# Bit masks in eight wide operations, one chunk's inverse over 128 partitions, a square on ScalarE, and a new stated order

## The chip, the cores and the metric

The kernel runs on one core of a Trainium2 chip. The metric is the device time of one execution in microseconds (us). The engines are PE (TensorE, matrix products; PEld is its weight load), DVE (VectorE), ACT (ScalarE), POOL (GpSimd) and SP (SyncE, which here only issues transfers).

## The reference

Delta-rule attention over 32 sequences (4 batches of 8 heads, 768 positions, head dimension 48), whose output, laid out as 4 x 768 x 384, passes through a normalised MLP with a residual:

```python
k_n = k / (np.linalg.norm(k, axis=-1, keepdims=True) + 1e-06)
for t in range(S):
    kt, vt, bt = (k_n[:, :, t], v[:, :, t], beta[:, :, t, None])
    y[:, :, t] = np.einsum('bhd,bhde->bhe', q[:, :, t], state)
    v_old = np.einsum('bhde,bhd->bhe', state, kt)
    state = state + bt[:, :, :, None] * np.einsum('bhd,bhe->bhde', kt, vt - v_old)
# x = y as (B, S, H*D), D = 384, hidden 1536
xn = (x - mu) / np.sqrt(var + 1e-06) * g_ln
out = x + np.maximum(xn @ w_ch1, 0.0) @ w_ch2
```

Everything is fp32.

## The kernel before

**Chunks.** The 768 positions are cut into 12 chunks of C = 64. Within a chunk the recurrence becomes matrix products, once a unit triangular 64 x 64 matrix, built from the products of the keys (`gram`, gsb) and beta, has been inverted for every head. The state then goes from chunk to chunk (`recur`: L979, L996 or L1013, L1020, L1030), and the chunk's 256 rows of output go through the MLP (`mlp`: first L1322 and L1337 for chunk 0, later L1296, L1217 and L1419).

**Two ways of inverting.** Chunk 0 is inverted by doubling (`first_inverse`): blocks of 1, 2, 4, ... 32 rows are joined in five levels. Each level, for each of two groups of heads, is a product E on PE (L720), a masked copy of its result on DVE (`copy_predicated`, L727), a product Z on PE (L737), two transposes on DVE (L685) and copies back on ACT (L679). The masks say which elements a level joins: one 128 x 64 mask for each of six bit numbers, made at the start on DVE from GpSimd's index ramps `xor` and `bits`. Before the levels, the norms of the keys are taken (`first_norms`: square L594, sum L595, square root L596, L597 to L602 for -beta / norm^2), the product of the keys is scaled by them (L693), masked (L702) and transposed (L708).

The other chunks are inverted by rows on DVE (`rows_inverse`), two chunks at a time with 128 partitions, one partition for each 32 x 32 block of each head; chunk 1 goes alone, on 64 partitions. Step j multiplies column j of the inverse by row j of the matrix (L856, into tmp) and subtracts (L863): 31 steps, with `n * w` elements each. The blocks come through DRAM (gsb to gd on SP, gd to gb, and at the end xb to xd and xd to xt); ACT and DVE take norms from the diagonal (L835 to L840) and scale (L846). Two 32 x 32 blocks are joined to 64 x 64 by `join` (transpose L884, products L894 and L900).

**Weights.** Both weight matrices come as 64-bit words in twelve pieces of 768 KB, fetched by ACT's queue into five buffers (`fetch`) and put together from their two halves by ACT (L524, L532), DVE (L529) and GpSimd (L542).

**The order.** Every step is recorded with `add` together with what it reads and writes. `emit` then writes the steps in the order of a list of step numbers, `ORDER`; a "z" in it stands for a matmul of zeros (L1511). Each engine executes its part of that list strictly in order (`in_this_order`), so an instruction that waits holds all behind it on its engine, transfers that it issues included.

```python
        for n in stated_order():
            if n < 0:
                self.filler()
                continue
            fn, deps = self.steps[n]
            fn()
```

ScalarE needs a table of functions for each set of activations; the build places a load in front of the first activation that needs another set. A square root of a constant (L439) is recorded early.

Of the kernel before, what the change touches and what calls it, by code (L numbers as in the profile page):

```python
# [9 lines left out]
I32 = mybir.dt.int32  # L10
# [6 lines left out]
C = 64  # L17
DP = 64
BK = 32
FB = 32  # L20
# [43 lines left out]
146 232 230 149 326 150 219 669 154 z 209 234 155 156 208 231 233 210 158 157 251 46 235 164 160 162 327 200 161 328 239 201 411 159 413 165 170 166  # L64
# [136 lines left out]
def kernel(  # L201
# [78 lines left out]
    masks = [small[:, i].bitcast(I32) for i in range(6)]  # L280
    xor, bits, eye, brow = small[:, 6].bitcast(I32), small[:, 7].bitcast(I32), small[:, 8], small[:, 9]
    bnat = sb("bnat", [128, GH])
    beta_f = sb("beta_f", [64, FB])
    beta_b = sb("beta_b", [128, NSL, BK])
    g_sb = sb("g_sb", [128, KC])
    eps = sb("eps", [128, 1])
# [843 lines left out]
    def cap(i):  # L1130
        return CAP[i]
# [517 lines left out]
```

## Time and profile before

| | |
|---|---|
| runs | 507.06, 510.91, 511.09 us (median 510.91) |
| profiled execution | 506.83 us, span 505.1 us |
| granted clock of PE, mean | 0.973 |
| busy: PE, PEld | 485.9 us (96%), 445.7 us (88%) |
| busy: DVE, ACT, POOL | 355.2 us (70%), 249.0 us (49%), 275.7 us (55%) |
| moved by transfers | 54.99 MB, 109 GB/s |
| costliest on DVE | L863 73.7 us (186 instructions), L856 73.1 us (186), L1237 63.6 us (96) |
| costliest on PE | L1419 109.5 and 84.5 us, L1296 50.2 us |

A stretch's row gives its length and then, for each engine, the busy time and the number of instructions, then PE's granted clock as a share of full speed and the busy share of the transfer engines. A row of the timeline gives start, duration, engine, line, operation, output and input, count, and in brackets the idle time before it with what ended it. Matmuls are pipelined, so that PE's busy time is the time in which something was in it.

### The profile page before, as it was taken

Reading aid. Unit: us, or ns where it says so; the run is one execution under the profiler, and the core shown is the slowest. Engines: PE = TensorE matmul, PEld = TensorE weight load, DVE = VectorE, ACT = ScalarE, POOL = GpSimd, SP = SyncE. Lnnn points to the kernel's source line nnn. Section 1 sums busy time; section 2 is a strip of 40 time slices with the busy share of each in tenths; the row PEclk is TensorE's granted clock in tenths of the full one; section 3 lists DMA queues with packets and bytes.
Section 4 is the critical chain, followed back from the end, with each engine's and each line's share of the span. In section 5 each row is a group of like instructions: output and inputs, shape, how many; then the busy total and the mean of one; then the engine's idle time right before and its main releaser. Section 6 shows DMA issues by size and latency. Waiting matters only on the chain.

```text
span 505.1 us, 22184 instructions
## 1 busy us (share of the span) xinstructions
PE 485.9 (96%) x9606; PEld 445.7 (88%) x9606; DVE 355.2 (70%) x774; ACT 249.0 (49%) x620; POOL 275.7 (55%) x430
## 2 busy tenths in 40 slices
PE   6777999999999999999999999999999999999996
PEld 3666988688988898899999999999999999999996
DVE  9689987997699458886559898478899238143251
ACT  5777772633645434636444544436563347363230
POOL 5464527255754595629893462591642851645643
PEclk9776799999999999999999999999999999999999
DMA  8979896756646676448734434765245412111101
GB/s 173 308 153 187 270 189 79 107 138 133 90 87 106 192 127 114 46 100 205 155 41 64 102 55 153 150 91 87 57 85 136 82 23 58 43 50 46 31 12 31
DMA packets 196097, 54.99 MB, mean 109 GB/s; under 512 B 186076, under 2 KB 189404, under 8 KB 196000
## 3 DMA queue, kind: packets, MB, share of 16 engines
q1 hardware_dynamic: 189920, 40.58, 42.1%
q10 hardware_dynamic: 3872, 9.83, 6.1%
q0 software_dynamic: 2208, 3.17, 3.7%
q8 instruction: 75, 1.23, 1.0%
q14 instruction: 22, 0.18, 0.1%
HBM read 36.64 MB, written 16.91 MB: 106 GB/s over the span
## 4 chain that ended last, share of the span: by engine, by line
PE 78%; DVE 13%; SPq 3%; issue 2%; POOL 1%; DMA 1%; ACT 1%; ACTq 0%; DVEq 0%; POOLq 0%
PE f L1419 31%; PE f L1217 22%; PE f L1296 6%; DVE xb L863 4%; DVE tmp L856 4%; SPq L349 3%; PE by L1020 2%; PE two L1013 2%; PE by L979 2%; PE by L771 2%; PE two L979 2%; PE two L1030 1%; PE two L771 1%; PE by L894 1%; PE by L900 1%
## 5 line engine op out<-in xcount | busy, mean ns | idle before, releaser
L1406 POOL TENSOR_TENSOR h_all<-h_all 128x256 f32<-128x256 f32 x123 | 90.2, 746 | 133.3 <-PE f L1419 103.7
L1419 PE MATMUL f<-w_sb,h_all 128*128 128x192 f32 x492 | 109.5, 332 | 0.0
L1419 PE MATMUL f<-words,h_all 128*128 128x192 f32 x396 | 84.5, 330 | 0.3 <-POOL h_all L1406 0.3
L1419 PEld LDWEIGHTS f<-w_sb,h_all 128*128 128x128 f32 x492 | 81.8, 190 | 1.8 <-DVE o L1437 0.2
L863 DVE TENSOR_TENSOR xb<-xb,tmp 128x87 f32<-128x87 f32 (+21 forms) x186 | 73.7, 396 | 4.8
L856 DVE TENSOR_TENSOR tmp<-xb,gb 128x87 f32<-128x87 f32 (+21 forms) x186 | 73.1, 393 | 4.9
L1237 DVE TENSOR_TENSOR h_all<-h_all,f 128x512 f32<-128x512 f32 x96 | 63.6, 682 | 14.2 <-PE f L1217 13.1
L1419 PEld LDWEIGHTS f<-words,h_all 128*128 128x128 f32 x396 | 66.6, 190 | 1.7 <-POOL h_all L1406 1.0
L1296 PE MATMUL f<-xnt,w_sb 128*128 128x256 f32 x216 | 50.2, 382 | 0.0
L349 POOL DMA_DIRECT2D tb<-in_k_dram x64 | 41.9, 660 | 10.3 <-DVE kt L751 9.4
L1239 ACT ACTIVATE h_all<-h_all 128x512 f32<-128x512 f32 x48 | 28.5, 624 | 34.4 <-DVE h_all L1237 34.0
L1296 PEld LDWEIGHTS f<-xnt,w_sb 128*128 128x128 f32 x216 | 40.2, 190 | 5.2
L1233 ACT COPY h_all<-f 128x512 f32<-128x512 f32 x48 | 26.3, 590 | 33.9 <-PE f L1217 17.1
L1437 DVE TENSOR_TENSOR o<-f,x 128x192 f32<-128x192 f32 x33 | 11.6, 352 | 41.8 <-PE f L1419 25.9
L1217 PE MATMUL f<-words,w_sb 128*128 128x128 f32 x256 | 31.7, 276 | 0.0
L1305 ACT ACTIVATE h_all<-f 128x256 f32<-128x256 f32 x36 | 13.4, 383 | 34.8 <-PE f L1296 34.8
L1217 PEld LDWEIGHTS f<-words,w_sb 128*128 128x128 f32 x256 | 30.0, 192 | 0.2
L1217 PE MATMUL f<-xnt,w_sb 128*128 128x128 f32 x192 | 25.4, 276 | 0.0
L542 POOL TENSOR_TENSOR w_sb<-words 128x768 uint32<-128x768 uint32 (+1 forms) x11 | 15.0, 1364 | 17.7 <-DVE words L529 16.7
L1217 PEld LDWEIGHTS f<-xnt,w_sb 128*128 128x128 f32 x192 | 23.7, 192 | 0.1
L1322 PEld LDWEIGHTS f<-xnt,w_sb 128*128 128x128 f32 x144 | 19.5, 203 | 3.4 <-ACT h_all L1330 0.2
L1084 ACT ACTIVATE xnt<-xnt,g_sb 128x256 f32<-128x256 f32 x27 | 12.5, 499 | 19.2 <-DMA xnt<-xld 19.1
(246 smaller groups left out, 955.0 us busy)
## 6 DMA issues: line engine op xcount, KB each, us to landing
words<-in_moe_w_ch_dram ACTq DMA_DIRECT2D x10, 768.0 KB, 7.8
gd<-gsb SPq DMA_DIRECT2D x11, 512.0 KB, 3.9
v<-in_v_dram SPq DMA_DIRECT2D x24, 192.0 KB, 4.2
kr<-in_k_dram SPq DMA_DIRECT2D x46, 96.0 KB, 3.9
out_dram<-o SPq DMA_DIRECT2D x44, 96.0 KB, 2.4
xld<-xlt SPq DMA_DIRECT2D x9, 384.0 KB, 3.0
xnt<-xld SPq DMA_DIRECT2D x36, 96.0 KB, 3.3
gb<-gd SPq DMA_DIRECT2D x44, 64.0 KB, 3.0
```

The source lines that it names most:

```text
L349: add(eng, cost, lambda: QUEUE[eng].dma_start(out=out_, in_=in_), r, w, bulk=n * ns / 16e3, **kw)
L856: lambda j=j, n=n, w=w, t=t: nc.vector.tensor_tensor(out=t, in0=xv[:, 0:n, j : j + 1].to_broadcast([np_, n, w]), in1=gv[:, j : j + 1, j + ...
L863: "DVE", dve(n * w), lambda t=t, rest=rest: nc.vector.tensor_tensor(out=rest, in0=rest, in1=t, op=ALU.subtract),
L979: nc.tensor.matmul(dst[half(e), hp, j], src[drows(hp), (e if n else key_half(c, hp, e)) * GP + j], s_all[drows(hp), e, j], start=(n == 0 o ...
L1217: nc.tensor.matmul(wide(p[:, 128 * n : 128 * n + 128]), w[n // 2][:, n % 2 * 128 : n % 2 * 128 + 128], r, start=start and n == 0, stop=Tru ...
L1233: add("ACT", act(512), lambda: nc.scalar.copy(o, p), pk, ok)
L1237: add("DVE", dve(512), lambda: nc.vector.tensor_tensor(out=o, in0=o, in1=p, op=op), pk, ok)
L1239: add("ACT", act(512), lambda: nc.scalar.activation(o, o, ACTF.Relu), [], ok)
L1296: nc.tensor.matmul(p[:, 0:TOK], w1_sb[:, t, f * 128 : (f + 1) * 128], xnt[:, t], start=(t == 0), stop=(t == KC - 1))
L1322: nc.tensor.matmul(p[:, 0:128], w1_sb[:, t, f * 128 : (f + 1) * 128], xnt[:, t, cols], start=(t == 0), stop=(t == KC - 1))
L1406: add(eng, cost, lambda: e.tensor_tensor(out=out_, in0=x, in1=y, op=op), r, w, port=2 if eng == "Pool" else 1, pr=-2)
L1419: lambda f=f, t=start and f == 0: nc.tensor.matmul(p[:, 0:D2], lhs(f), rhs[:, f], start=t, stop=(f == F2 - 1), skip_group_check=True),
```

## The change

Four parts. Code lines that are only moved are left out.

**Masks.** The two index ramps are laid out so that one 32-bit word holds a column's or row's own bits in its upper half and the exclusive-or in its lower half; a shift by the bit number, an AND and a compare then give a mask. Mask 0 is made by itself, masks 1 to 5 together on 320 columns.

**Chunk 1 on 128 partitions** (`ways=2`): partitions 64 to 127 hold a second copy of the 64 blocks; of the inverse's rows the even ones are kept in the lower and the odd ones in the upper half, so a step has about half the elements. The second copy comes by one transfer gb to gb, and beta for it by two more loads, issued on ACT's queue. The result goes back by eight transfers instead of four.

**Norms:** (norm + 1e-6)^2 is an activation with a bias on ACT instead of a product on DVE.

**Order:** `ORDER` is another list throughout.

```diff
-    beta_f = sb("beta_f", [64, FB])
+    beta_f = sb("beta_f", [128, FB])
...
+    rows_, both, steps = flat[:, 960:1024], flat[:, 832:960].rearrange("p (n t) -> p n t", t=C), flat[:, 800:806]
+    wide = flat[:, 0 : 6 * C].rearrange("p (n t) -> p n t", t=C)
+    c_pool(lambda: nc.gpsimd.iota(steps, pattern=[[1, 6]], base=0, channel_multiplier=0), 0.15, ["steps"])
...
-    for n in MASKED:
-        k_, m, w = n, masks[n], C
-        t1, t2 = (flat[:, C * i : C * i + w] for i in (2 * n, 2 * n + 1))
...
-                out=t1, in0=xor[:, 0:w], scalar1=w - 1, scalar2=k_, op0=ALU.bitwise_and, op1=ALU.logical_shift_right
...
-                out=t2, in0=own, scalar1=k_, scalar2=1, op0=ALU.logical_shift_right, op1=ALU.bitwise_and
...
-                out=m, in0=t1, scalar=1, in1=t2, op0=ALU.is_equal, op1=ALU.mult
...
+    for n, (own, key) in enumerate(((bits, "bits"), (rows_, "rows"))):
...
+                out=both[:, n], in0=own, scalar=16, in1=xor, op0=ALU.logical_shift_left, op1=ALU.bitwise_or
...
+    for n in range(2):
+        ns_ = slice(0, 1) if n == 0 else slice(1, 6)
...
+                out=wide[:, ns_], in0=both[:, n : n + 1].to_broadcast([128, m_, C]),
+                in1=steps[:, ns_, None].to_broadcast([128, m_, C]), op=ALU.logical_shift_right,
...
+                out=wide[:, ns_], in0=wide[:, ns_], scalar1=65536 + C - 1, scalar2=None, op0=ALU.bitwise_and
...
+                out=small[:, ns_].bitcast(I32), in0=wide[:, ns_], scalar1=65537, scalar2=None, op0=ALU.is_equal
...
             add("ACT", 0.21, lambda ss=ss, nr=nr: nc.scalar.sqrt(nr, ss), ks, kn_, **kw)
+            add("ACT", 0.21, lambda nr=nr, nd=nd: nc.scalar.activation(nd, nr, ACTF.Square, bias=eps), kn_ + ["eps"], kd, **kw)
             add("DVE", 0.17, lambda nr=nr: nc.vector.tensor_scalar_add(nr, nr, 1e-6), [], kn_, port=2, **kw)
-            add("DVE", 0.17, lambda nr=nr, nd=nd: nc.vector.tensor_tensor(out=nd, in0=nr, in1=nr, op=ALU.mult), kn_, kd, port=1, **kw)
...
-    def rows_inverse(L, chunks, beta_l, xd, **kw):
-        np_ = C * len(chunks)
-        gv, xv, tv = gb[0:np_], xb[0:np_], tmp[0:np_]
+    def rows_inverse(L, chunks, beta_l, xd, ways=1, **kw):
+        own = C * len(chunks)
+        np_, LA = own * ways, L // ways
+        gv, xv, tv = gb[0:np_], xb[0:np_, 0:LA], tmp[0:np_]
...
+        if ways > 1:
+            dma("SP", gb[own:np_], gb[0:own], own, 168, [("gb", n) for n in range(4)], [("gb", 4)], **kw)
...
+        for q in range(ways):
+            pq = slice(own * q, own * q + own)
...
+                    out=xv[pq].rearrange("p s t -> p (s t)")[:, q :: L + ways], in_=db[pq, q::ways]
...
-            n, w = j + 1, L - 1 - j
+            n, w = j // ways + 1, L - 1 - j
...
+            for q in range(ways):
+                dma(
+                    "SP", xts[c % NX][rows.start + q : rows.stop : ways, :, cols],
+                    xdv[own * q + p0 : own * q + p0 + GH].rearrange("h s t -> s h t"),
...
+    for e in range(2):
+        dma(
+            "ACT", beta_f[C + e * FB : C + (e + 1) * FB],
+            beta[2 * e : 2 * e + 2, :, C : 2 * C].rearrange("g h (b t) -> b (g h) t", t=FB),
...
-    rows_inverse(FB, (1,), (beta_f, [("beta_f", e) for e in range(2)]), 1, pr=-20)
+    rows_inverse(FB, (1,), (beta_f, [("beta_f", e) for e in range(4)]), 1, ways=2, pr=-20)
```

What the new order does on the engines in the front part of the program:

- ACT: before, the only table load stands in front of L439, which is ACT's first activation. Now a load stands in front of the first copy L426 and another in front of the first square root L596, and L439 comes after the two new squares. The first fetch of weights follows the second L596 instead of preceding both.
- DVE: mask 0 and the two `both` words come before the sums L595, the shift and AND for masks 1 to 5 after them, their compare after the second group's L708. L846 comes after the last L727 of the first group instead of ahead of it.
- PE: E of the second group (L720) comes ahead of Z of the first (L737) in the first level; the eight transposes of the queries come after the second level's first product; the third level's first product comes ahead of the second level's last. There are two zero products instead of one, and the eight transposes of chunk 3's keys (L568) stand ahead of the first L1322 instead of behind it.
- POOL: the identity matrix is finished after the beta loads and two memory operations; the second beta row is loaded after both beta_f parts.
- SP: the transfer gb to gb follows the four loads gd to gb of chunk 1, ahead of three loads of chunk 2's keys.

More of the change, by code (lines that the diff above doesn't have):

```diff
@@ L386 @@
     )
-    c_dve(
-        lambda: nc.vector.tensor_tensor(out=flat[:, 960:1024], in0=xor, in1=bits, op=ALU.bitwise_xor), 0.22, ["rows"], ["xor", "bits"], port=1,
-    )
     MASKED = (0, 1, 2, 3, 4, 5)
-    for n in MASKED:
-        k_, m, w = n, masks[n], C
-        t1, t2 = (flat[:, C * i : C * i + w] for i in (2 * n, 2 * n + 1))
+    for n, (own, key) in enumerate(((bits, "bits"), (rows_, "rows"))):
         c_dve(
-            lambda t1=t1, k_=k_, w=w: nc.vector.tensor_scalar(
-                out=t1, in0=xor[:, 0:w], scalar1=w - 1, scalar2=k_, op0=ALU.bitwise_and, op1=ALU.logical_shift_right
+            lambda n=n, own=own: nc.vector.scalar_tensor_tensor(
+                out=both[:, n], in0=own, scalar=16, in1=xor, op0=ALU.logical_shift_left, op1=ALU.bitwise_or
@@ L397 @@
             ),
-            0.17, [("ma", n)], ["xor"], port=2,
+            0.22, [("both", n)], [key, "xor"], port=1,
         )
-        own = flat[:, 960 : 960 + w] if n else bits[:, 0:w]
+    for n in range(2):
+        ns_ = slice(0, 1) if n == 0 else slice(1, 6)
+        m_ = ns_.stop - ns_.start
         c_dve(
-            lambda t2=t2, k_=k_, own=own: nc.vector.tensor_scalar(
-                out=t2, in0=own, scalar1=k_, scalar2=1, op0=ALU.logical_shift_right, op1=ALU.bitwise_and
+            lambda n=n, ns_=ns_, m_=m_: nc.vector.tensor_tensor(
+                out=wide[:, ns_], in0=both[:, n : n + 1].to_broadcast([128, m_, C]),
+                in1=steps[:, ns_, None].to_broadcast([128, m_, C]), op=ALU.logical_shift_right,
@@ L404 @@
             ),
-            0.18, [("mb", n)], ["bits", "rows"], port=2,
+            0.08 + 0.07 * m_, [("ma", n)], [("both", n), "steps"], port=1,
         )
         c_dve(
-            lambda m=m, t1=t1, t2=t2: nc.vector.scalar_tensor_tensor(
-                out=m, in0=t1, scalar=1, in1=t2, op0=ALU.is_equal, op1=ALU.mult
+            lambda ns_=ns_: nc.vector.tensor_scalar(
+                out=wide[:, ns_], in0=wide[:, ns_], scalar1=65536 + C - 1, scalar2=None, op0=ALU.bitwise_and
             ),
-            0.22, [("mask", n)], [("ma", n), ("mb", n)], port=1,
+            0.1 + 0.04 * m_, [("ma", n)], [], port=2,
@@ L412 @@
         )
-    MASK_SCRATCH = [(x, n) for x in ("ma", "mb") for n in MASKED] + ["rows"]
+        c_dve(
+            lambda ns_=ns_: nc.vector.tensor_scalar(
+                out=small[:, ns_].bitcast(I32), in0=wide[:, ns_], scalar1=65537, scalar2=None, op0=ALU.is_equal
+            ),
+            0.1 + 0.04 * m_, [("mask", k) for k in range(ns_.start, ns_.stop)], [("ma", n)], port=2,
+        )
+    MASK_SCRATCH = [("ma", 0), ("ma", 1), ("both", 0), ("both", 1), "rows", "steps"]
     BEGIN = [(kts[2], "kt", 2), (gsbs[2], "g", 2), (gsbs[3], "g", 3), (xts[2], "xt", 2), (xts[3], "xt", 3), (pts[1], "pt", 1)]
@@ L842, in rows_inverse @@
         )
-        add("Pool", 0.25, lambda: nc.gpsimd.tensor_copy(out=diag(xv), in_=db), ["db_b"], ["xb"], **kw)
+        for q in range(ways):
+            pq = slice(own * q, own * q + own)
+            add(
+                "Pool", 0.25,
+                lambda q=q, pq=pq: nc.gpsimd.tensor_copy(
+                    out=xv[pq].rearrange("p s t -> p (s t)")[:, q :: L + ways], in_=db[pq, q::ways]
+                ),
+                ["db_b"], ["xb"], **kw,
+            )
         add(
```

29 lines of the change are left out of this document (17 added, 12 removed), and 180 rows, old and new, of the table ORDER.

## The prediction

> **What bounds the kernel now.** I read first the table of stretches (busy time by engine, TensorE's granted clock, DMA share), cut where the chain of the first chunk passes: first row product (L693, 11.15), second level of the doubling (20.89), its last product (42.67), first MLP matmul (L1322, 53.14).
>
> ```profile
> core 0: us, PE busy (x) PEld busy (x) DVE busy (x) ACT busy (x) POOL busy (x), PEclk, DMA share, GB/s
> 0.00:11.15 11.15, 8.04 (x94) 4.44 (x94) 10.06 (x39) 5.33 (x12) 6.60 (x17) 1.00 0.86 163
> 11.15:20.89 9.74, 7.45 (x202) 6.23 (x204) 6.28 (x13) 8.01 (x20) 2.60 (x4) 0.68 1.12 301
> 20.89:29.30 8.41, 5.15 (x203) 4.83 (x200) 5.67 (x11) 5.74 (x15) 5.56 (x10) 0.70 0.81 214
> 29.30:42.67 13.37, 9.27 (x308) 7.23 (x303) 12.71 (x33) 9.29 (x24) 6.84 (x10) 0.88 0.90 226
> 42.67:53.14 10.47, 9.25 (x259) 8.21 (x260) 9.36 (x24) 8.63 (x22) 6.25 (x7) 0.50 0.85 148
> 53.14:56.00 2.86, 2.86 (x20) 2.74 (x24) 2.76 (x7) 1.78 (x4) 2.10 (x2) 0.56 0.84 237
> 56.00:123.00 67.00, 67.00 (x1272) 55.00 (x1270) 57.26 (x132) 33.89 (x95) 31.41 (x43) 1.00 0.72 147
> ```
>
> From 56 us on PE is never idle; before that it is, and runs part of the time at half clock. The waits of PE after 57 us say the same of the rest of the program:
>
> ```profile
> PE f L894 <- DVE xnj L884: 0.4, 1, 0.4
> PE f L1419 <- POOL h_all L1406: 0.3, 1, 0.3
> PE f L894 <- issue: 0.3, 1, 0.3
> ```
>
> So 1.0 us is all that 448 us of stream can give back. The chain of work that ended last names DVE's L856 and L863 (8% of the span), but PE has other work beside them. The change pays only by how much earlier PE's closed stream begins. In the front these rows of the timeline count (lines are numbered as in the kernel before throughout):
>
> ```profile
> 2.26 1.28 ACT L439 ACT_TABLE_LOAD   x1 [2.26 <-issue]
> 3.80 2.38 DVE L402 TENSOR_SCALAR xb<-xb 128x64 int32<-128x64 int32 x1
> 5.93 0.52 ACT L594 ACTIVATE xln<-kr 128x384 f32<-128x384 f32 x1 [2.18 <-DMA kr<-in_k_dram]
> 8.10 0.54 DVE L595 TENSOR_REDUCE ksum<-xln 128x8 f32<-128x384 f32 x1
> 9.23 0.31 ACT L596 ACTIVATE knrm<-ksum 128x8 f32<-128x8 f32 x2 [1.37 <-DVE ksum L595]
> 11.15 0.68 DVE L693 TENSOR_TENSOR gsb<-two,ndb 128x512 f32<-128x512 f32 x1
> 18.29 0.94 POOL L827 MEMSET xb<- 64x1024 f32 x1 [10.64 <-DVE u L408]
> 24.58 0.39 PE L771 MATMUL f<-qt,kt 48*64 48x64 f32 x10 [2.41 <-issue]
> ```
>
> Read: L402 takes 2.38 us, while an undisturbed one takes 0.18, because it runs beside GpSimd's copies; so the sum of squares (L595) begins at 8.10 though its square ended at 6.45. The sequencer of PE stops 2.41 us at 22.17 for nothing the profile shows.
>
> **Masks.** Twenty-two DVE instructions become eleven. Ten of these lie before the reductions or in ScalarE's wait behind them. The five later masks fell to fifteen operations of 0.18 to 0.21 (2.9 us); three of 320 columns replace them. Shift: 0.41 (L856 at 252 columns) to 0.55 (L1001, 384); AND and compare: 0.34 (L529, 384) as the upper end, 0.20 (64 columns) as the lower. Together 0.8 to 1.25; I take 1.05. The reductions can then start with their squares, at 6.45 and 7.39: 1.3 us earlier for the second (ended 9.20, now 7.9).
>
> **Norms and a second table load.** The dummy square root that loaded ScalarE's table at 2.26, in idle time, now stands behind the real ones. The built program has two loads instead of one: one in front of the first copy (L426), one directly in front of the first square root (L596). The second costs 1.28 by its row, at the place where the masks were just taken away. ScalarE's queue then reads: second square ends 7.39, load 8.67, square root 8.87, a copy of 512 (0.53) 9.4, two key copies (1.07) 10.5, square root 10.7, a DMA issue (0.37) 11.05, the two new squares (0.31) 11.4. DVE: two reciprocals (0.20) and two scalings (0.17), 12.1. So L693 begins at 12.1, 0.9 us later than 11.23 when its wait ended; without the load it would be 10.8. The new squares replace L598 (0.16 on DVE) and put L597 off the path, which the load outweighs. Three moves hide behind it: GpSimd selects the identity at about 6.4 (done at 3.7 before; first transposes at 5.96, their copies now wait till 9.4); the second beta row is issued at about 5.3 instead of 3.67 and, at 3.6 to land, is there at 9 for a product that now comes at 10.6; the first weight fetch goes from 7.04 to 10.7 and lands, at the median 7.8, at 18.5, where ScalarE may wait up to 1 us for it, with 2 us until the second level needs its copies.
>
> The Trainium skill (ScalarE: Activation LUTs, What ACT_TABLE_LOAD costs) gives a switch of sets 1283 ns and a drain of 1380 ns besides; the row agrees with the first, and no row here has a load behind running work. By the page L693 would begin at 13.5 and the sum below would be 1.4 us worse.
>
> **Doubling.** The first level in the new order, by rows: L693 0.61, L597 0.16, L702 0.74, L708 0.72 (14.35); the same for the second group (16.5), the wide compare 0.3, L727 0.73 (17.5), product Z at half clock 1.13 (18.6), L685, L727, L685 1.6 (20.2). The eight query transposes (1.97) no longer stand between; a zero matmul (0.6 a piece) does, and Z of the second group ends at 20.8. The second level starts at 20.8; before 20.89. Even.
>
> From there to the last product of the first group DVE decides. Its instructions in the new order: six L727 of 0.70 and one of 0.43, twelve L685 of 0.40, L529 four times 0.34 and twice 0.55, L802 1.25, one memset 0.27, norms of chunk 1 about 1.2: 14.6 us. From the result of the second level (21.6) this ends at 36.2, if DVE never waits. Before, the same place was reached at 42.5: L846 (1.2) and seven operations of the pair loop (1.5) stood ahead, PE stopped 2.41, and the third level waited for both groups of the second. In the new order L846 is behind, and the third level's first product is ahead of the second level's last.
>
> **The inverse of chunk 1.** Columns times rows per pass fall from 5456 to 2856 elements; at 1.04 ns each (60 columns 0.214, 252 columns 0.414) two passes save 5.4 us of DVE between 40 and 70 us. PE is full from 48 on, so this alone is worth nothing there; what hides it is MLP 0, and chunk 1 is not asked for until 84.62 (L894).
>
> It adds transfers. One copies 256 KB from 64 partitions to the other 64 and must wait for four loads from gd. Before, these were issued until 27.73; a median of 3.0 to land gives 31; issue 0.6, and landing 3.5 (xd, same size): 35. Only then may L835 run, in ScalarE's queue ahead of the last level's copies back, and L836 to L840 in DVE's, ahead of L727 of the fourth level's second group. L840 also needs beta_f, whose last part is now issued on ScalarE's queue at about 32; with 3.8 to 4.9 to land that is 36 to 37. So DVE is held about 1 to 2 us: last product at 37.9 instead of 36.4. On SP three loads of keys stand behind that copy and shift some 3 us, their transposes (38.02) hardly. The four extra stores (0.49 each) come after 65 us, hidden like the rest. ScalarE's two new issues cost 0.37 each.
>
> **Sum.** Last product at 36.4 to 40.3 (the upper end with a stop like the 2.41 again); I take 38.8 against 42.67: 3.9 earlier. The 10.47 to L1322 I keep: its chain is the same, and the transposes moved ahead of L1322 are only exchanged for the same ones behind. Of the 1.0 us of waits after 57 I take back 0.4. The profiled execution took 506.83 (span 505.1, 1.7 around it): 502.5. The median shown, 510.91, is 4.1 above that execution; two of the four executions stand at 507 and two at 511, so I add 2.3: **504.8 us**. Its own range, without the rivals, is 499 to 509.
>
> **Rivals.** *Given back to the clock, no change:* the granted clock fell to a half at 14.7, 25.0 and 42.1 and came back at 21.5, 31.8 and 55.7, always multiples of about 3.4 us apart. The last return followed 7.3 us of closed work (from 48.4). Each such step of closed work at half clock costs 1.7. If it returns two steps later relative to the work, 3.4 of the 3.9 are lost, and the stops of PE may eat the rest: 508 to 511. For: it is the same front with a zero matmul more, and 507 against 511 looks like two such steps; against: the work is denser. The Trainium skill (TensorE: Matmul & The Clock Gate, Part 1) calls this window 3.4 us and free-running, which the distances agree with; it follows that the step may fall either way in each execution.
>
> *Slower, the copy between partitions holds both queues:* should the loads take as long as the store before them (16.21 issued, read at 23.63: 7.4), the last lands at 35.8 and the copy, at the weights' 7.8, at 44.2; L727 behind L840 is then at 45.5 against 37.85, 7.7 later, and some 1.5 come back from the shorter loop: 6 slower, 513 to 517. It decides from L840 ending after 37.85, only 1.2 behind my 36.6. For: the DMA share is 0.8 to 1.1 there; against: the median landing of gb is 3.0.
>
> *More:* no stop of PE and the clock back one step earlier: last product 36.4, 1.7 besides: 8 faster, 496 to 499.
>
> **Chances.** Forecast 0.50, clock 0.26, slower 0.17, more 0.07. One per cent, about what a measurement of this kernel can tell from no change, is 5.1 us of 510.91. Below 505.8 lie 0.35 of the forecast's 0.50 and the last rival's 0.07: 0.42. Within it lie the forecast's other 0.15 and 0.25 of the clock's 0.26: 0.40. Slower: 0.17 of the third case and 0.01 of the clock's: 0.18. The range 498 to 514 leaves out about 0.2, half of the slower and of the larger case among it.
>
> **What would show it.** Right: two table loads, the second at about 7.4; L595 at 6.5; L693 at 12; the last L737 of the first group before 40; L1322 before 51 with PE closed behind it; L863 on half the elements, its loop ending before 65. Wrong: L835 idle behind a DMA past 37 us, PE idle over 2 us after 57, or a half clock reaching past 56.

## The result and the profile after

| | before | changed |
|---|---|---|
| median of 21 runs each | 509.38 us (506.47 to 511.89) | 514.03 us (509.49 to 515.77) |
| ratio, 95% interval | | 1.0081 (1.0061 to 1.0101) |
| profiled execution, span | 506.83 us, 505.1 us | 511.96 us, 509.9 us |

The change costs 0.8%, some 4 us. The forecast was 504.8 us, faster, within 498 to 514. Ratios here and below are taken over all fast runs (one slow run each of y2_late and x4_shift is left out) and are not quotients of the medians.

The profiled execution of the changed kernel is one of its quicker ones, and its mean granted clock, 0.972, is high for it: the mean over the 21 executions is 0.9665, against 0.9726 over the 120 executions of the kernel before in the experiments below. In the traces the clock is either full or half, so this means 34.2 us at half clock on average against 27.8.

Lines below are those of the changed kernel. What the prediction calls L595, L596, L693 is now L602, L603, L700; E (L720), Z (L737), masked copy (L727), transpose (L685), copy back (L679) are L727, L744, L734, L692, L686; L835, L856, L863 are L845, L874, L881; L884 and L894 are L905 and L915; L949, L1092 are L970, L1113; L996, L1001, L1020 are L1017, L1022, L1041; L1322 and L1419 are L1343 and L1440.

The table of stretches, cut at the same places of the chain: first row product, second level, third level, last product of group 0, first MLP product.

```profile
core 0: us, PE busy (x) PEld busy (x) DVE busy (x) ACT busy (x) POOL busy (x), PEclk, DMA share, GB/s
0.00:11.78 11.78, 9.12 (x88) 4.79 (x89) 6.51 (x25) 6.90 (x14) 5.34 (x17) 1.00 1.01 140
11.78:19.74 7.96, 5.58 (x202) 4.41 (x205) 6.56 (x14) 7.20 (x16) 3.26 (x7) 1.00 1.00 358
19.74:26.77 7.03, 3.21 (x120) 2.67 (x112) 2.96 (x8) 3.23 (x11) 1.16 (x2) 1.00 0.93 267
26.77:44.45 17.68, 13.93 (x386) 11.90 (x390) 11.59 (x26) 11.64 (x28) 10.29 (x13) 0.50 0.84 180
44.45:57.67 13.22, 10.96 (x285) 9.79 (x280) 12.51 (x32) 10.98 (x29) 7.71 (x8) 0.63 0.94 168
57.67:123.00 65.33, 62.96 (x1196) 51.06 (x1196) 56.07 (x133) 33.98 (x94) 32.76 (x45) 1.00 0.67 145
```

The third level begins at 26.77, 2.5 us earlier than before (29.30). The next two cuts are late: 44.45 against 42.67, and 57.67 against 53.14. From 26.9 to 54.2 PE ran at half clock without a break, and from 57.67 to 123 it is no longer closed: 2.4 us of it are idle, where before it was busy for all of 56 to 123. The waits of PE name the places.

```profile
engine line waited for: us in total, times, longest us
PE f L744 <- issue: 3.4, 1, 3.4
PE by L727 <- ACT xt L686: 2.1, 3, 0.9
...
PE two L727 <- issue: 1.4, 1, 1.4
...
PE f L1343 <- ACT h_all L1351: 0.6, 1, 0.6
PE f L915 <- DVE xnj L905: 0.6, 1, 0.6
```

Two stops of PE's own sequencer (4.8 us; the two longest before 2.9) and three waits for ScalarE's copies back stand in the front; the last two rows, and three of 0.4 to 0.5 like them, make the holes behind it.

The front itself came out as forecast. ScalarE, then VectorE, from the timeline:

```profile
7.03 0.52 ACT L601 ACTIVATE xln<-kr 128x384 f32<-128x384 f32 x1
7.57 1.28 ACT L603 ACT_TABLE_LOAD   x1
8.86 0.21 ACT L603 ACTIVATE knrm<-ksum 128x8 f32<-128x8 f32 x1
```

```profile
6.65 0.55 DVE L602 TENSOR_REDUCE ksum<-xln 128x8 f32<-128x384 f32 x1 [1.62 <-ACT xln L601]
...
11.78 0.68 DVE L700 TENSOR_TENSOR gsb<-two,ndb 128x512 f32<-128x512 f32 x1
```

The second table load stands where it was expected and takes its 1.28; the square root follows 0.01 us behind it.

From the third level on, PE's timeline shows what took the time:

```profile
30.77 1.13 PE L744 MATMUL f<-xt,xt 64*64 64x64 f32 x30 [0.54 <-ACT xt L686]
32.84 1.13 PE L727 MATMUL by<-qt,gsb 64*64 64x64 f32 x32 [0.94 <-ACT xt L686]
33.75 1.08 PE L778 MATMUL f<-qt,kt 48*64 48x64 f32 x32
34.76 1.22 PE L1538 MATMUL f<-ident 128*128 128x256 f32 x2
35.91 0.70 PE L727 MATMUL two<-qt,gsb 64*64 64x64 f32 x15
37.97 0.70 PE L727 MATMUL two<-qt,gsb 64*64 64x64 f32 x16 [1.36 <-issue]
```

The last two rows are product E of the fourth level, group 0. VectorE's transposes for it ended at 33.1, but in PE's list the third level's E of group 1, a query product and a product of zeros stand ahead, each at half clock, and the sequencer stops in the middle of it. From the third level's E (26.77) to the last part of the fourth's it took 11.2 us; before, 5.7:

```profile
29.30 1.08 PE L720 MATMUL two<-qt,gsb 64*64 64x64 f32 x32
...
34.99 0.69 PE L720 MATMUL two<-qt,gsb 64*64 64x64 f32 x30 [1.06 <-DVE qt L685]
```

### The profile page after: what moved, and what is told of

Same layout as the page of the kernel before. It is cut to its first block, busy times and chain, and to the rows that moved or that the text cites. A ratio compares the mean times of both kernels' runs of the same rounds, so it can differ in the third digit from the quotient of the medians.

```text
span 509.9 us, 22184 instructions
## 1 busy us (share of the span) xinstructions
PE 488.1 (96%) x9608; PEld 446.2 (88%) x9608; DVE 353.8 (69%) x761; ACT 248.9 (49%) x623; POOL 274.9 (54%) x432
## 3 DMA queue, kind: packets, MB, share of 16 engines
q8 instruction: 75, 1.23, 1.0%
## 4 chain that ended last, share of the span: by engine, by line
PE 74%; DVE 10%; SPq 3%; issue 2%; DMA 2%; POOL 2%; ACT 1%; DVEq 0%; ACTq 0%; POOLq 0%
PE f L1440 28%; PE f L1238 22%; PE f L1317 6%; DVE tmp L874 4%; DVE xb L881 4%; SPq L349 3%; PE by L1041 2%; PE two L1034 2%; PE by L1000 2%; PE two L1000 2%; PE by L778 2%; PE two L1051 1%; POOL h_all L1427 1%; PE two L778 1%; PE by L915 1%
## 5 line engine op out<-in xcount | busy, mean ns | idle before, releaser
L1427 POOL TENSOR_TENSOR h_all<-h_all 128x256 f32<-128x256 f32 x123 | 89.8, 741 | 130.6 <-PE f L1440 71.7
L1440 PE MATMUL f<-w_sb,h_all 128*128 128x192 f32 x492 | 108.1, 331 | 0.0
L1440 PE MATMUL f<-words,h_all 128*128 128x192 f32 x396 | 85.4, 330 | 0.1
L1440 PEld LDWEIGHTS f<-w_sb,h_all 128*128 128x128 f32 x492 | 82.3, 190 | 1.5
L874 DVE TENSOR_TENSOR tmp<-xb,gb 128x87 f32<-128x87 f32 (+23 forms) x186 | 79.4, 427 | 4.7
L881 DVE TENSOR_TENSOR xb<-xb,tmp 128x87 f32<-128x87 f32 (+23 forms) x186 | 71.2, 383 | 4.8
L1440 PEld LDWEIGHTS f<-words,h_all 128*128 128x128 f32 x396 | 66.7, 190 | 1.8 <-POOL h_all L1427 0.6
L1317 PEld LDWEIGHTS f<-xnt,w_sb 128*128 128x128 f32 x216 | 40.1, 190 | 6.9 <-ACT xnt L1128 1.1
L1458 DVE TENSOR_TENSOR o<-f,x 128x192 f32<-128x192 f32 x33 | 11.5, 354 | 38.8 <-PE f L1440 27.3
L1079 ACT ACTIVATE x<-by 128x384 f32<-128x384 f32 x23 | 11.2, 487 | 29.3 <-PE by L1041 19.5
L1238 PEld LDWEIGHTS f<-xnt,w_sb 128*128 128x128 f32 x192 | 23.8, 192 | 0.2
L549 POOL TENSOR_TENSOR w_sb<-words 128x768 uint32<-128x768 uint32 (+1 forms) x11 | 14.9, 1357 | 16.8 <-DVE words L536 7.9
L1343 PEld LDWEIGHTS f<-xnt,w_sb 128*128 128x128 f32 x144 | 18.4, 192 | 4.5 <-ACT h_all L1351 1.0
```

Source lines behind the costliest of these rows:

```text
L874: lambda j=j, n=n, w=w, t=t: nc.vector.tensor_tensor(out=t, in0=xv[:, 0:n, j : j + 1].to_broadcast([np_, n, w]), in1=gv[:, j : j + 1, j + ...
L881: "DVE", dve(n * w), lambda t=t, rest=rest: nc.vector.tensor_tensor(out=rest, in0=rest, in1=t, op=ALU.subtract),
L1238: nc.tensor.matmul(wide(p[:, 128 * n : 128 * n + 128]), w[n // 2][:, n % 2 * 128 : n % 2 * 128 + 128], r, start=start and n == 0, stop=Tru ...
L1317: nc.tensor.matmul(p[:, 0:TOK], w1_sb[:, t, f * 128 : (f + 1) * 128], xnt[:, t], start=(t == 0), stop=(t == KC - 1))
L1343: nc.tensor.matmul(p[:, 0:128], w1_sb[:, t, f * 128 : (f + 1) * 128], xnt[:, t, cols], start=(t == 0), stop=(t == KC - 1))
L1427: add(eng, cost, lambda: e.tensor_tensor(out=out_, in0=x, in1=y, op=op), r, w, port=2 if eng == "Pool" else 1, pr=-2)
```

## The experiments

The first theory was that the new order is to blame: the places in PE's and ScalarE's queues just shown, and the table load. The rivals were the parts (their transfers), the clock, and the stops. Every ratio is against runs of the kernel before on the same chip, whose median lay between 508.6 and 509.5.

### Parts and order apart

x1_parts has the new code in the old list of steps, x2_order the old code in the new list:

```diff
 x1_parts: ORDER
-the changed kernel's list
+the list before; beta's two loads behind L799 and behind a weight fetch, the gb-to-gb copy behind its four loads
 x2_order: ORDER
-the list before
+the changed kernel's list
```

> The three new parts (wide masks, chunk 1's inverse by parity, squares on ScalarE) in the old order; the two added loads of beta stand on ScalarE's queue behind the second copy of chunk 1's key products and behind the weight fetch of 29.7 us. Theory 'order' (the list of steps, not the parts, costs the time): the time of the kernel before or up to 3 us less, 506 to 510; one table load; MLP 0's first matmul at 51 to 53.5. Rival 'parts' (the added transfers and loads hold a queue or the transfer engines): 3 to 6 us slower than before, 512 to 515, with a wait on the 256 KB copy visible on ScalarE or VectorE between 31 and 45 us.

> The old parts (22 mask operations, chunk 1 on 64 partitions, products of the norms on VectorE) in the new order; of the old masks' operations 10 stand where the wide shift and AND stand and 5 where the wide compare stands. Theory 'order': slower than before by as much as the whole change or more, 4 to 9 us: 513 to 518, since about 1.9 us of narrow mask operations come back onto VectorE's path and 5.4 us of the longer pair loop. Rival 'parts': within 1 us of before.

x1_parts: 512.62 us, ratio 1.0074 (1.0048 to 1.0100). x2_order: 518.69, 1.0185 (1.0152 to 1.0217). The first came out as the rival 'parts' had it, the second as 'order' had it and a little worse, and neither theory had both: the parts cost as much as the whole change, and the new order without them costs twice as much. In x1_parts the rival of the prediction is to be seen, PE waiting for a transpose that waits for ScalarE:

```profile
35.32 0.28 PE L727 MATMUL two<-qt,gsb 64*64 64x64 f32 x2
39.58 1.12 PE L727 MATMUL two<-qt,gsb 64*64 64x64 f32 x30 [3.98 <-DVE qt L692]
```

ScalarE stood still for 4.88 us, until 38.63, ahead of L845, the square root of chunk 1's diagonal. By the program L845 waits for the 256 KB copy, issued at 31.03; the profile names no releaser. Does this wait make the 3.8 us?

```diff
 x5_parts_late: ORDER of x1_parts
-L845 ahead of the fourth level's copies back (ACT); L846 to L850 among its transposes (DVE)
+L845 behind them; L846 to L850 behind its last masked copy
 x6_masks: x1_parts
-rows_inverse(FB, (1,), ..., 1, ways=2, pr=-20)
+rows_inverse(FB, (1,), ..., 1, pr=-20)
```

> All three parts in the old order as in x1_parts, but chunk 1's square root on ScalarE stands behind the copies back of the fourth level, and the four operations on VectorE behind it stand behind the masked copy of the fourth level's second group. Theory 'held queue': the 2.8 us wait of ScalarE before the fourth level's copies is gone, and the time is 3 to 5 us under x1_parts: 507.5 to 509.5. Rival 'stops and clock': within 1.5 us of x1_parts, 511 to 514.

> Only the wide masks and the squares on ScalarE, in the old order; chunk 1's inverse on 64 partitions as before. The parts together in the old order took 512.6 us, 3.8 over before. Theory 'held queue' (there the square root of the diagonal waits on ScalarE for the 256 KB copy and holds the copies back of the fourth level for 2.8 us; masks and squares cost nothing): before's time or up to 2 us less, 506.5 to 509.5. Rival 'stops and clock' (moving the front at all shifts TensorE's stops and its half clock to a worse place): 510 to 513.

x5_parts_late: 512.74, 1.0080 (1.0047 to 1.0112): the wait is gone and the time is the same. x6_masks: 509.02, 0.9994 (0.9967 to 1.0020): masks and squares are worth nothing. So in the old order the split of chunk 1 costs the 0.7 to 0.8%, and not by that wait.

### The split in the new order

```diff
 x7_nosplit: the changed kernel
-rows_inverse(FB, (1,), ..., 1, ways=2, pr=-20)
+rows_inverse(FB, (1,), ..., 1, pr=-20)
```

> The new order with the wide masks and the squares on ScalarE, but chunk 1's inverse on 64 partitions as before. The old parts in the new order took 518.7 us, with a wait of TensorE of 4.2 us near 75 us for VectorE's normalisation, which stood behind the longer pair loop. Theory 'the split pays in the new order, and only there': the same wait of 3 to 5 us, 517 to 519.5. Rival 'the masks pay': no such wait, 513 to 515.5.

518.47 us, 1.0179 (1.0148 to 1.0210), like x2_order with its old masks and squares. In the new order the same split is worth 1.0179 against 1.0081, some 5 us. VectorE's timeline says why; first x7_nosplit, then the changed kernel:

```profile
77.17 0.20 DVE L881 TENSOR_TENSOR xb<-xb,tmp 64x31 f32<-64x31 f32 x1
77.29 0.55 DVE L536 TENSOR_SCALAR words<-words 128x768 uint32<-128x768 uint32 x1
77.76 0.41 DVE L970 TENSOR_SCALAR xln<-x,mv 128x384 f32<-128x384 f32 x1
```

```profile
72.12 0.19 DVE L881 TENSOR_TENSOR xb<-xb,tmp 128x16 f32<-128x16 f32 x1
72.23 0.56 DVE L536 TENSOR_SCALAR words<-words 128x768 uint32<-128x768 uint32 x1
72.70 0.41 DVE L970 TENSOR_SCALAR xln<-x,mv 128x384 f32<-128x384 f32 x1
```

The new list puts the MLP's second normalisation (L970) behind the whole of chunk 1's loop. The loop ends 5.05 us earlier with the split (the prediction's 5.4), and PE's wait for L970, 3.3 us by the waits of x7_nosplit, shrinks to 0.4 in the changed kernel:

```profile
PE by L1113 <- DVE xln L970: 3.3, 1, 3.3
```

### Mending the front

```diff
 x3_load: ORDER, ACT
+L446 (square root of a constant) first of all activations
 L433, L601, L433, L601, L603, ...
-L446 behind L604
 y2_late: ORDER
+copies back and transposes of the last level's group 1, its E (L727) and masked copy ahead of L1017
+L1022, L1041 ahead of L575 (keys of chunk 2)
 y4_all: x3_load and y2_late, and
 L727 by (third level, group 1)
+L727 two (fourth level, group 0)
 L778 f (query products)
 L1538 f (zeros)
-L727 two (fourth level, group 0)
+second and third levels' copies back (L686) ahead of the conversions (L531, L539) that stood between
```

> The changed kernel with one step moved: the square root of a constant stands first on ScalarE again, so that there is one table load in idle time and none in front of the first square root. Rival 'table load' (its 1.28 us, doubled by the clock and the stops behind it, is what makes the kernel slower): the front is 1.2 us earlier to the scaled key products (10.6 in place of 11.78) and the time falls by 3 to 5 us, to before's or below. Theory 'order': the front is 1.2 us earlier, but the half clock and the queue behind the fourth level stay: 0 to 1.5 us faster than the changed kernel, still 3 us slower than before.

> The changed kernel with group 1 of the last doubling level moved ahead: its copies back and transposes, its product E and its masked copy stand ahead of the first group's product with v, and the product with u ahead of the transposes of the keys of chunk 2. In the changed kernel the product with u waits until 52.45 us, because VectorE's scaled difference stands behind a masked copy that waits for E of group 1, which began at 48.23. Theory 'late chain': the product with u begins at 48 to 49.5, the first MLP product at 53.5 to 55 (57.67 before), and the time falls by 2.5 to 4 us: 510 to 511.5. Rival 'clock' (TensorE's half clock until 54 us sets the front whatever the order): the product with u moves, the first MLP product does not by more than 1 us, and the time stays within 1 us of the changed kernel's 514.

> The changed kernel with four moves and nothing else: the table load in idle time, the product E of the fourth level's first group straight behind E of the third level's second group (ahead of the query products and the product of zeros), the second and third levels' copies back ahead of the weight conversions on ScalarE, and group 1 of the last level ahead as in y2_late. Theory 'order' (these queue places are what made it slower): E of the fourth level begins at 33 to 34 in place of 35.9, the first MLP product at 50 to 53, and the time is 505 to 509: at before's or below. Rival 'clock and stops': the first MLP product at 55 or later, 511 to 514.

x3_load: 513.70, 1.0092 (1.0063 to 1.0120). y2_late: 515.01, 1.0102 (1.0067 to 1.0137). y4_all: 513.39, 1.0077 (1.0051 to 1.0103). No mending reached the end. In x3_load the row products came at 10.60 as expected, 1.2 us earlier, and then:

```profile
17.20 0.36 PE L727 MATMUL by<-qt,gsb 64*64 64x64 f32 x1 [1.14 <-issue]
...
20.60 1.10 PE L727 MATMUL two<-qt,gsb 64*64 64x64 f32 x32
```

The second level began at 20.60, later than the 19.74 of the changed kernel: the sequencer stopped for 1.14, and the clock had fallen to a half at 15. In y4_all the chain moved as asked:

```profile
32.90 1.08 PE L727 MATMUL two<-qt,gsb 64*64 64x64 f32 x32
...
49.88 1.11 PE L1041 MATMUL two<-u,pt 64*64 64x48 f32 x32 [0.72 <-DVE u L1022]
...
58.22 1.58 PE L1343 MATMUL f<-xnt,w_sb 128*128 128x128 f32 x12
```

E of the fourth level came 3.0 us earlier, the product with u 2.6, the first MLP product 0.6 later. The transposes of keys and queries, the last Z and the products of chunk 2's keys have to go through PE first in either case, at half clock until 55. Over the first 62 us PE's busy time is 47.3 us in y4_all, 47.1 in the changed kernel, 48.0 before, all at a mean clock of 0.78.

```diff
 x8_nozero: ORDER of x6_masks
-z (L1538, between the third level's E of group 0 and of group 1)
```

> x6_masks (509.0 us) without the one product of zeros in the third level, which lies 1.22 us at half clock ahead of the product E of the second group. Theory 'chain' (the front's chain sets the start of the stream): 1 to 1.5 us less, 507.5 to 508. Rival 'closed work' (TensorE's lost time in the front is the same whatever stands in the chain, since the clock and other waits take it back): within 0.7 us of x6_masks.

509.87 us, 1.0006 (0.9982 to 1.0030), against x6_masks' 0.9994: taking 1.22 us of PE out of the chain gains nothing either. In its profile PE is 1.0 to 1.9 us ahead of x6_masks, step by step, between 40 and 100 us, and 0.4 behind it at the end.

### Front and stream apart

The first 320 steps of the two lists hold the same steps but for nine. So either front can be joined to either stream:

```diff
 h1_front:  new list to step 320, then the rest in the order of x5_parts_late
 h2_stream: x5_parts_late to step 320, then the rest in the new order
 h3_mended: y4_all to step 320, then the rest in the order of x5_parts_late
```

> All three parts. Up to the first MLP product (320 steps) the new order; from there on the old order, as in x5_parts_late. The two prefixes hold the same steps but for nine. Theory 'front' (what is lost is lost before 62 us): the changed kernel's time, 513 to 515. Theory 'stream' (the new order behind the front lets TensorE wait 2.4 us between 62 and 123 us, where the old one lets it wait 0): 2 to 2.5 us less, 511 to 512.

> All three parts. Up to the first MLP product the old order as in x5_parts_late, then the new one. Theory 'front': x5_parts_late's time or up to 1 us less, 511.5 to 513. Theory 'stream': 2 to 2.5 us over x5_parts_late, 514.5 to 515.5, with waits of TensorE of 2 us or more between 62 and 123 us.

> The front of y4_all (one table load, the fourth level's product and group 1 of the last level ahead, copies ahead of conversions), then the old order. Theory 'stream': 2 us under y4_all, 511 to 512; theory 'front': 513 to 514; both leave it slower than the kernel before's 508.6. Should the mended front and the old stream add up better than either theory says: 509 or less.

h1_front: 513.09, 1.0078 (1.0050 to 1.0106). h2_stream: 512.30, 1.0060 (1.0038 to 1.0083). h3_mended: 513.84, 1.0094 (1.0061 to 1.0126). All three lie where theory 'front' put them and none where 'stream' did. The test is not clean, though: in the profile of h1_front the waits of PE between 62 and 123 us are gone (busy for 61.00 of 61 us, in the changed kernel 58.63), but its front, the changed kernel's by its list, stood still for 20.5 of the first 62 us instead of 14.9, with four stops of the sequencer that come to 7.2 us instead of 4.8. The changed kernel and all kernels with the split whose steps are only ordered otherwise, in the old order, the new one or a mixture, lie between 1.0060 and 1.0102, with intervals that overlap. With the split in place, the order is not what costs.

### What in the split costs

Four kernels on the base of x6_masks, with L845 to L850 placed late as in x5_parts_late: that base alone, and one part of the split at a time; and x5_parts_late with beta brought otherwise.

```diff
 s0_base: nothing added
 s1_copy:
+dma("SP", gb[own:2 * own], gb[0:own], own, 168, [("gb", n) for n in range(4)], [("gb", 4)], **kw)
 s2_beta:
+dma("ACT", beta_f[C + e * FB : C + (e + 1) * FB], ...)   # e = 0, 1
 s3_stores:
-dma("SP", xts[...][rows, :, cols], xdv[p0 : p0 + GH] ...)
+dma("SP", xts[...][rows.start + q : rows.stop : 2, :, cols], xdv[p0 : p0 + GH, q::2] ...)   # q = 0, 1
 s4_nobeta: x5_parts_late
-dma("ACT", beta_f[C + e * FB : C + (e + 1) * FB], ...)
+dma("SP", beta_f[own:np_], beta_f[0:own], ...)   # behind the gb copy
```

> The old order with wide masks and squares (x6_masks, 509.0 us, the time of the kernel before), chunk 1 still inverted on 64 partitions, plus one part of the split alone: the 256 KB copy to the other 64 partitions, with chunk 1's square root waiting for it as late as in x5_parts_late (512.7). Theory 'copy' (its 4 to 8 us in the transfer engines delay the loads behind it): 2 to 4 us over x6_masks, 511 to 513. Rivals 'beta' and 'loop': within 1 us of x6_masks, 508 to 510.

> The same base plus only the two added loads of beta, issued on ScalarE's queue at about 15 us (1.2 us of issuing, in a stretch where ScalarE has no gap) and at about 30 us (0.7). Theory 'beta' (they delay ScalarE's copies and fall into TensorE's stop for instructions, which took 1.3 to 2.8 us in four kernels without these loads and 2.0 to 4.0 in nine with them): 1.5 to 4 us over x6_masks, 510.5 to 513. Rivals 'copy' and 'loop': within 1 us of it, 508 to 510.

> The same base plus only the eight transfers instead of four that bring chunk 1's inverse back. Theory 'stores' (four more issues of 0.5 us on SP's queue and rows of half the number delay the loads of keys behind them): 1 to 3 us over x6_masks. All other theories: within 1 us of it, 508 to 510.

> x5_parts_late (all parts, 512.7) with the second copy of beta made by one 8 KB transfer on SP behind the 256 KB one instead of the two loads on ScalarE's queue. Theory 'beta': 1.5 to 4 us under x5_parts_late, 509 to 511, with TensorE's stop near 22 us at 1.3 to 2.8. Rivals 'copy', 'stores' and 'loop': within 1 us of x5_parts_late, 511.7 to 513.7.

> The base of s1_copy, s2_beta and s3_stores with none of the three added: wide masks and squares in the old order, chunk 1 on 64 partitions, its square root, the four operations behind it and its scaling placed later as in x5_parts_late. The three lay 0.27 to 0.34% over the kernel before. Theory 'three small costs' (each added transfer costs 1.2 to 1.5 us, and together they are the 3.7): the time of before, 508.3 to 509.3. Rival 'later place' (the later place of chunk 1's square root costs it, and the transfers cost nothing, so that the shorter loop must cost the rest): 510 to 510.5.

| | median us | ratio, 95% interval |
|---|---|---|
| s0_base | 508.87 | 0.9989 (0.9963 to 1.0016) |
| s1_copy | 510.09 | 1.0034 (1.0010 to 1.0057) |
| s2_beta | 510.09 | 1.0027 (1.0005 to 1.0049) |
| s3_stores | 510.48 | 1.0034 (1.0010 to 1.0059) |
| s4_nobeta | 512.33 | 1.0065 (1.0039 to 1.0091) |

No single transfer is the culprit. The base is as fast as the kernel before; each of the three additions is slower than before by some 0.3%, 1.4 to 1.7 us. The three together, 0.95%, are enough for the 0.7 to 0.8% that the split costs in the old order. That the shares simply add is not shown, nor what the shorter loop gives back there: no run has two of the additions, or the loop without them. Against s0_base itself the intervals just overlap at their ends, so the single sizes are not sharp. s4_nobeta gives back 0.15%, in keeping with one such share and within its error.

By what each share is lost is not shown, but the places can be narrowed down. The kernel before, x1_parts, x5_parts_late, x6_masks and the five here give PE the same 9606 products in the same order (a handful of neighbours swap places in the records). Product by product, their profiles come apart from s0_base's by -2.5 to 3.3 us before 60 us, by 1.6 to 2.3 us more near 140 us in five of them, by some 1 us near 95 us in two, and by no more than 0.4 us behind 148 us. The profiles of s2_beta and s3_stores have a wait of PE of 1.6 us near 141 us that s0_base and s1_copy have not, behind a transfer xt<-xd that VectorE (L905) waits for: 2.1 and 2.5 us against 0.3 and nothing. But x6_masks and x8_nozero, as fast as the kernel before, have it too (3.0 and 3.1). One profiled execution is too few for 1.5 us. The clocks of all executions show one thing more: s1_copy, s2_beta and s3_stores spend 6.0, 3.8 and 2.6 us more at half clock than the kernel before on the same chip (each uncertain by 2.3 to 3.2), s0_base does not (1.6 less). Whether the shares are lost by this is not shown.

### The stops of the sequencer

```diff
 x4_shift: fill(), first call only
     nc.tensor.matmul(ps[:, 0:cols], nought, ...)
+    for _ in range(32):
+        nc.tensor.matmul(ps[:, 0:8], nought, nought[:, 0:1].to_broadcast([128, 8]))
```

> The changed kernel with 32 products of zeros of 8 columns each (64 records of TensorE) added to the first filling, while TensorE has nothing else to do. In both kernels TensorE stopped for 1.4 to 3.4 us, with nothing shown as the cause, behind the records numbered about 346 and 602. Theory 'instruction index' (the stop belongs to a fixed number of instructions): the stops come behind the same numbers counted with the added 64, so 64 of the old records earlier: in the first level's products Z (about 18 to 20 us) and in the third level's E. Rival 'place' (the stop belongs to what runs there, or to a time or transfer): they stay in Z of the second level and in E of the fourth, at 22 and 36.6 us. The time: within 2 us of the changed kernel under both.

527.18 us, 1.0328 (1.0286 to 1.0369), so the forecast of the time missed: the 32 narrow products took 13.66 us instead of hiding. PE is 12.0 us behind the changed kernel at the second level (31.78 against 19.74) and 7.6 at the first MLP product (65.23 against 57.67); behind that come a stop of 3.62 us at 72.22 and half clock again from 71.7 to 78.5. What the kernel asks is told by the stops all the same. In its rows L784, L750 are L778, L744 of the changed kernel:

```profile
26.93 0.27 PE L784 MATMUL f<-kt 48*64 48x64 f32 x1 [1.14 <-issue]
...
33.49 0.81 PE L750 MATMUL f<-xt,gsb 64*64 64x64 f32 x32
...
52.67 0.85 PE L750 MATMUL f<-xt,pt 64*64 64x32 f32 x18 [0.22 <-issue]
```

The product that was cut in two by 3.4 us in the changed kernel (Z of the second level) now runs through in one row, which answers the rival 'place'. Counted over PE's list of products, the stops stood behind records 220, 346 or 347, 474 or 475, 601 or 602, 728 and 855 in kernels of either order (347 is the stop of 2.41 shown in the prediction), in x4_shift behind 221, 856 and 1237 with the 64 counted: 127 apart, or a multiple of it, within two. So a stop can come only at such an end; the theory's own ends, 346 and 602, passed without one in x4_shift. The profile's page, here of the changed kernel, shows that instructions come by transfers:

```profile
span 509.9 us, 22184 instructions
...
q8 instruction: 75, 1.23, 1.0%
q14 instruction: 22, 0.18, 0.1%
```

The columns are packets, MB and share. 1.23 MB in 75 packets are 16.4 KB each; 1.41 MB for 22184 instructions are about 64 bytes each; so a packet is some 256 instructions, 128 pairs of weight load and product. The 75 packets of q8 hold 19200 instructions, and PE has 19216 products and weight loads: q8 brings PE's. The trace's records of transfers give the time of each packet:

| | PE stood still (us) | packet moved | from its end to PE's next product |
|---|---|---|---|
| before | 22.17 to 24.58 | 22.35 to 23.22 | 1.36 |
| changed | 22.04 to 25.43 | 23.17 to 24.13 | 1.30 |
| x1_parts | 21.67 to 25.65 | 23.34 to 24.27 | 1.38 |
| s3_stores | 22.32 to 26.03 | 23.59 to 24.47 | 1.56 |
| x4_shift | 68.60 to 72.22 | 69.86 to 70.82 | 1.40 |

All 49 stops of the sequencer over 0.3 us in the first 75 us of the twenty profiles end 1.2 to 1.8 us behind such a packet. So PE stops at the end of a block whose successor is not there yet. The stop at 346 or 347 took 1.3 to 4.0 us in all profiles but x4_shift's. That the added loads of beta lengthen it fell with s3_stores, which has none of them and 3.7 us.

The Trainium skill (Runtime: NRT & Kernel Launch, Instruction fetch mechanics) describes this refill in blocks of 16 KiB or 256 instructions, with which packets and distances agree; it also holds the fetch to be hidden behind the issue of instructions, and in this front it is not.

## Why the prediction was wrong

**Right: the front to the second level.** Reductions at 6.65 (6.5 forecast), table load at 7.57 (7.4), row products at 11.78 (12.1), three wide operations 1.09 us (1.05), second level at 19.74 (20.8; the forecast had counted product Z at half clock, and PE's clock was full up to 26.9). That masks, squares and load together are worth nothing held: x6_masks 0.9994, x3_load no faster than the changed kernel. The drain of 1380 ns that the Trainium skill (ScalarE: Activation LUTs, What ACT_TABLE_LOAD costs) adds to a load did not show behind running work: ScalarE went on 0.01 us after the 1.28.

**Wrong: "from there to the last product of the first group DVE decides".** The sum of VectorE's work was about right, 14.6 us: it is busy 2.96 + 11.59 = 14.55 in the two stretches from 19.74 to 44.45, 0.7 of it a scaling that the forecast had behind. But these are 24.7 us, and it stood idle for 10, so the last product of the first group came at 44.45 instead of 38.8. PE was the bound, in its order and at half clock, with products of the other group, of queries and of zeros between the links of the chain, and with 4.8 us of stops for instructions. The forecast allowed for one such stop only at its upper end, 40.3.

**Wrong: "the 10.47 to L1322 I keep", and with it the whole sum.** It took 13.22 us (44.45 to 57.67). And even where the chain was made earlier by 2.6 to 3 us (y4_all) or relieved of 1.22 (x8_nozero), the time did not follow. Up to the first MLP product PE has a fixed amount of other work, which the chain only shares PE with. The better measure is PE's lost time up to a fixed amount of its work, and in the profiled pair this hardly moves in the front: of the first 62 us PE is idle 14.0 before and 14.9 after, and the half clock lasts 27.3 us in both. What the profiled execution loses more comes behind it, 2.4 us of holes up to 123 us for a start; idle time of PE over 2 us after 57 was one of the prediction's own signs of being wrong.

**Mis-sized: the split's transfers, priced at nothing because MLP 0 hides them.** Added alone to the old order they cost 0.3% each (s1_copy, s2_beta, s3_stores), 1.4 to 1.7 us, enough together for the 3.8 to 4.1 us that the split costs there. That they cost as much in the new order is not shown, since no run takes them out of it and leaves the loop. That they hold VectorE 1 to 2 us was wrong, and so was the rival: in the changed kernel L845 comes at 41.23, straight behind the copy back ahead of it and 11.3 us after the 256 KB copy was issued (the longest landing on record is 8.3). The rival's mechanism exists in x1_parts, and taking it away there changed nothing.

**Wrong place: "this alone is worth nothing there".** In the old order the split as a whole costs time, shorter loop included; in the new one, which stands on the loop, it is worth some 5 us: without it the new order costs 1.8%.

**The clock rival** had the size about right (no gain), and more of its mechanism came than the profiled pair shows. There the half clock only lies elsewhere, 26.9 to 54.2 in one piece instead of three. But over all executions it lasts 6.5 us longer in the changed kernel (34.2 against 27.8), about the two steps of 3.4 that the rival counted; if PE was busy throughout, that is an estimated 3.2 us. It is not the whole cause: x1_parts, h2_stream and y4_all have only 1.0 to 1.7 us more of it than the kernel before and are 3.2 to 3.9 us slower. The chance of a slower kernel, 0.18, rested on one mishap, the copy; all the new transfers should have stood there.

What remains open is by what three small transfers cost 1.4 to 1.7 us each, a wait or a longer half clock, and why the new order without the split loses more than the 3.3 us at L970 (x7_nosplit has 9.4 us more at half clock than the kernel before, x2_order 3.5).

## What to carry to other kernels

A chain of waits says what ended last, not what the end is worth: where PE has other work that must be done before its closed stream begins, count PE's lost time up to the same amount of work, and take time off the chain as a gain only if that falls. A transfer beside a full engine isn't free for being off the path; price it by adding it alone to the old kernel. Read the granted clock over all executions before you say that it did not change; one profile can be a lucky one. When parts and order are changed together, measure the parts in the old order and the old parts in the new one: here one part paid for the order, and neither was worth having.

## What was not expected of the hardware

PE stops at the ends of blocks of some 128 pairs, by up to 4.0 us in the front and by 0.4 to 1.1 us near 142 to 152 us in twelve kernels, while the next 16.4 KB of instructions are fetched. The count of instructions says where a stop can fall, and the packet's arrival whether one does. A product of zeros with 8 columns (a pair of records) takes 13.66 / 32 = 0.43 us, against 1.9 for one with 512 in the same filling: here 32 narrow fillers cost as much as seven wide ones. The 256 KB copy between partitions took 8.3 us to land in x5_parts_late and 3.5 in h2_stream, which have the same list up to there.
